# A gated mix of local attention and a spectral filter on one core: each engine's order planned anew

## The chip, the cores and the metric

The kernel runs on one core of a Trainium2 chip. The metric is the device time of one execution in microseconds (us), the median of several. The profile is of one execution; its times are in us from the first instruction. The engines are named as in the profile: PE (TensorE) multiplies matrices and PEld is its loading of weights, DVE (VectorE) and POOL (GpSimd) do elementwise work and reductions, ACT (ScalarE) copies, scales and takes exponentials, SP (SyncE) issues transfers.

## The reference

```
g = sigmoid((x * gate_w).sum(-1))                       # x: 1 x 2048 x 640, float32
a = attention(x @ wqkv) @ wo                            # 32 heads of 20; row s sees rows s, s-2, ..., s-14
b = irfft2(rfft2(x) * (w_r + 1j * w_i))                 # over rows and columns
return g * a + (1 - g) * b
```

The attention is over eight rows at distance two, with a softmax; rows before the start are masked.

## The kernel before

The 2048 rows are laid out as 128 partitions by 16 columns j, row 16p + j. Attention at distance two couples only columns of one parity, so even and odd j are two halves (`par` 0 and 1).

**Products of the input.** `qkv(par, hg)` multiplies eight column blocks of x, turned, by a quarter of `wqkv`. Each float32 factor is split into a rounded high part and a remainder, `hi` and `lo`, and three products are added. The names are `xe` and `xo` for the split x of even and odd j, `st` for the raw x of the first ones, `raw` and `w` for the weights before and after the split. ACT makes `hi`, DVE or POOL the `lo`. ACT evacuates the sums to `ev`, and its queue stores them in `qkvd` in device memory.

**Attention.** `attend(par, h)` loads `kt`, `q` and `vt` for a half of four heads, multiplies q by eight shifted rows of k (`pr`, on DVE with q copied to PSUM by ACT as `qbank`, or for some on POOL), reduces (`L`), takes the softmax, multiplies by v on POOL (`pv`), reduces on DVE (`o`) and stores to `od`.

**Spectral filter.** `fold(q)` loads x as `fx` and folds its columns on DVE; `cols` makes the first transform over rows (`z`). `freq(g)` runs for 16 groups of frequencies: `u` and `v` on PE, their sum and difference `ab` on DVE, `xa` to `xd` on PE, the filter on POOL (`P`) and DVE (`p`, `xd`, then `s`), and `g` on PE. The chain of one group on DVE is p, two operations on xd, two on s, each reading the one before. `spatial(j)` makes the way back (`oa`, `ob`, `ha`, `hb`, `y`).

**Projection.** `project_even` and `project_odd` load `ot` from `od`, turn it on PE (`oTp`), split it (`oT`) and multiply by `wo` into `woa` and `wob`, 15 products each. The even ones go by device memory (`ad`, read again as `yi`); the odd ones are the last work of the kernel, with the store of `out`.

**The order.** No engine's order is written out by hand. Every call on an engine is recorded by the class `Plan` (`record`, line 222) with its reads and writes (`touch`, line 188), and at the end `issue` (line 463) hands the calls out in the order that `order` (line 276) found. So all work is issued from L636 in the profile. `cost` (line 241) gives each operation its booked time `busy` and a latency `lat`. `forward` (line 411) is a simulated run in which each engine takes, of the operations that are ready, the one with the longest remaining path (`tail`). `backward` (line 369) recomputes `tail` from the end of that run. `turns` (line 315) repeats both, and `late` (line 329) judges an order by its end under three draws of random delays. `order` then tries 60 sets of tails with random shifts, one shift for each tile's name, and keeps the best. On the chip each engine runs its line strictly in the order found and waits for data where it isn't there.

Transfers are booked by a common link of 380 GB/s (`RATE`), a ring of 250 GB/s for each issuing engine (`QUEUE`) and a latency `LAND`. A load of an input may not start before `early`, which is 130 us (`AHEAD`) ahead of the time that its remaining path calls for. An operation behind one that it reads, on the same engine, is booked without a pause.

Of the kernel before, what the change touches and what calls it, by code (L numbers as in the profile page):

```python
# [139 lines left out]


class Op:
    __slots__ = ("i", "eng", "name", "call", "busy", "lat", "size", "preds", "succs", "chain", "tail", "start", "end", "early", "group", "of", "two")


class Engine:
# [9 lines left out]
class Plan:  # L156
# [31 lines left out]
    def touch(self, op, ap, write):  # L188

        if not hasattr(ap.tensor, "tag"):  # L190
            return
        tag, name = ap.tensor.tag, ap.tensor.name
        place = self.places.setdefault(tag, [name, {}, set()])
        if place[0] != name:
            assert name not in self.past, f"{name} used again after {place[0]}"
            self.past.add(place[0])
            self.places[tag] = place = [name, {}, {acc[0] for page in place[1].values() for acc in page}]
        pages, before = place[1:]
        if write:
            op.preds |= before  # L200
        p0, p1, idx = self.region(ap)
        size = PAGE if p1 > 1 else 1 << 30
        for pg in np.unique(idx // size):
            mine = idx[idx // size == pg]
            lo, hi, dense = mine[0], mine[-1], len(mine) == mine[-1] - mine[0] + 1
            kept = []
            for acc in pages.get(pg, ()):
                o, w, q0, q1, alo, ahi, adense, aidx = acc
                hit = o is not op and q0 < p1 and p0 < q1 and alo <= hi and lo <= ahi
                if hit and not (dense and adense):  # L210
                    hit = len(np.intersect1d(mine, aidx, assume_unique=True)) > 0
                if hit and (w or write):
                    op.preds.add(o)
                covered = write and hit and p0 <= q0 and q1 <= p1
                if covered:
                    covered = lo <= alo and ahi <= hi if dense else len(np.setdiff1d(aidx, mine, assume_unique=True)) == 0
                if not covered:
                    kept.append(acc)
            kept.append((op, write, p0, p1, lo, hi, dense, mine))
            pages[pg] = kept  # L220

    def record(self, eng, name, fn, a, k):
        op = Op()
        op.i, op.eng, op.name, op.chain, op.group = len(self.ops), eng, name, self.chain, self.group
        op.preds, op.succs, op.size, op.early, op.two = set(), [], 0, False, False
        line = sys._getframe(2).f_lineno
        code = self.code.get(line)
        if code is None:
            code = self.code[line] = compile("\n" * (line - 1) + "fn(*a, **k)", __file__, "exec")
        op.call = (code, {"fn": fn, "a": a, "k": k})  # L230
        aps = [v for v in list(a) + list(k.values()) if hasattr(v, "tensor") and hasattr(v, "ap")]
        out = k["out"] if "out" in k else a[0]
        ins = [v for v in aps if v is not out]
        for v in ins:
            self.touch(op, v, False)
        self.touch(op, out, True)
        op.of = out.tensor.name
        self.cost(op, out, ins, k)
        self.ops.append(op)

    def cost(self, op, out, ins, k):
        n = max(int(np.prod(v.shape[1:])) for v in [out] + ins[:1])
        if op.name == "dma_start":
            op.busy, op.lat = {"SP": 0.45, "ACT": 0.45, "POOL": 1.0}[op.eng], LAND
            op.size = int(np.prod(out.shape)) * 4
            op.early = not hasattr(ins[0].tensor, "tag")
        elif op.eng == "PE":
            n = int(np.prod(out.shape[1:]))
            if op.name == "transpose":
                op.busy = 0.109  # L250
            elif ins[-1].dtype == F32R:
                op.busy = n / 2400 + 0.018
            else:
                op.busy = 4 * n / 2400 + 0.006
            op.lat = 0.25
        elif op.eng == "DVE":
            op.busy, op.lat = 0.075 + n / 960, 0.12
            two = sum(v.tensor.tag[:4] not in ("bank", "qban") for v in ins) == 2
            if op.name == "scalar_tensor_tensor":
                op.busy += 0.06  # L260
            elif op.name == "reciprocal":
                op.busy += n * 0.007
            elif two:
                op.two = True
        elif op.eng == "ACT":
            strided = any(len(v.ap) > 2 and v.ap[-1][0] > 1 for v in [out] + ins)
            op.busy, op.lat = 0.12 + n * (1.75e-3 if strided else 0.78e-3), 0.15
            if len(ins) > 1:
                op.busy += 0.1
        else:  # L270
            spread = any(v.ap[-1][0] == 0 for v in ins)
            op.busy, op.lat = 0.09 + n * (2e-3 if spread else 2.25e-3), 0.14
        if op.eng in ("DVE", "ACT", "POOL") and not op.size:
            op.busy *= PACE

    def order(self):
        ops = self.ops
# [14 lines left out]
            last[key] = op  # L292
        span = max(op.tail for op in ops)
        for op in ops:
            op.early = max(0.0, span - op.tail - AHEAD) if op.early else 0.0
            op.tail += BIAS.get(op.chain, 0.0)
        rng = np.random.default_rng(SEED)
        self.draws = [rng.exponential(size=len(ops)).tolist() for _ in range(DRAWS)]
        best = self.turns(TURNS)

        names = {n: i for i, n in enumerate(dict.fromkeys(op.of for op in ops))}
        family = np.array([names[op.of] for op in ops])
        for _ in range(AGAIN):
            move = MOVE * rng.choice([0.3, 1.0, 2.0]) * rng.normal(size=len(names))
            move *= rng.random(len(names)) < rng.choice([0.1, 0.5, 1.0])
            for op, t in zip(ops, (best[1] + move[family]).tolist()):
                op.tail = t
            best = min(best, self.turns(2), key=lambda b: b[0])
        self.ends = best[0], best[3]
# [19 lines left out]
    def late(self, order, draw):  # L329

        line = {e: [op for op in order if op.eng == e] for e in ENGS}
        at, free, rings, link = dict.fromkeys(ENGS, 0), dict.fromkeys(ENGS, 0.0), dict.fromkeys(ENGS, 0.0), 0.0
        over, out = {}, {}
        head = {}
        last = 0.0
        for _ in range(len(order)):
            for e in ENGS:
                if head.get(e) is None and at[e] < len(line[e]):
                    op = line[e][at[e]]
                    t = free[e]  # L340
                    for q in op.preds:
                        if q not in out:
                            break
                        t = max(t, over[q] if q.eng == e and not q.size else out[q])
                    else:
                        head[e] = t
            e = min((h for h in ENGS if head.get(h) is not None), key=lambda h: head[h])
            op, t = line[e][at[e]], head.pop(e)
# [4 lines left out]
            over[op] = free[e] = end = t + busy  # L353
            if op.size:
                link = max(link, end) + op.size / RATE
                own = rings[e] = max(rings[e], end) + op.size / QUEUE
                end = (own if own >= link else min(link, own + op.size / QUEUE)) + SOONEST + LATER_BY * late
            else:
                end += op.lat - LATE.get(op.chain, 0.0)
            out[op] = end  # L360
# [3 lines left out]

    @staticmethod
    def lag(op, s):
        return 0.0 if s.eng == op.eng and not op.size else op.lat + EDGE.get((op.eng, s.eng), 0.0)

    def backward(self, end):

# [40 lines left out]
    def forward(self):  # L411
# [1 line left out]
        lat = self.lag  # L413
        wait = {op: len(op.preds) for op in ops}
        ready, pend = {e: [] for e in ENGS}, {e: [] for e in ENGS}
        free, rings, link = dict.fromkeys(ENGS, 0.0), dict.fromkeys(ENGS, 0.0), 0.0
        for op in ops:
            op.start = op.early
            if not wait[op]:
# [2 lines left out]
        while len(done) < len(ops):  # L422
# [26 lines left out]
            free[e] = op.end = op.start + op.busy  # L449
            avail = op.end  # L450
            if op.size:
                link = max(link, op.end) + op.size / RATE
                own = rings[e] = max(rings[e], op.end) + op.size / QUEUE
                avail = own if own >= link else min(link, own + op.size / QUEUE)
            done.append(op)
            for s in op.succs:
                wait[s] -= 1
# [9 lines left out]
                exec(*op.call)  # L467


TURNS, AGAIN, MOVE, SEED = 6, 60, 2.0, 2  # L470
DRAWS, SOONEST, LATER_BY = 3, 2.4, 0.6
ENGS = ("PE", "DVE", "ACT", "POOL", "SP")
RATE = 380e3
QUEUE = 250e3
LAND = 3.2
LATE = {"w": 1.0, "f": 4.0, "x": 3.5, "swap": 1.5}
AHEAD = 130.0
WAIT = 1.3
PACE = 1.02
EDGE = {("POOL", "ACT"): 2.0, ("DVE", "ACT"): 1.0}  # L480
LOOK = {"PE": 0.1, "DVE": 0.3, "ACT": 0.2, "POOL": 0.3, "SP": 0.0}
BIAS = {"first": 5.0, "logits": -5.0}
# [694 lines left out]
```

## Time and profile before

| | |
|---|---|
| median of 3 runs | 467.32 us (467.08 to 467.43) |
| span of the profiled execution, first to last instruction | 465.3 us |
| busy PE, DVE, POOL, ACT | 457.0, 423.4, 323.9, 205.2 us |
| moved by transfers | 105.90 MB, mean 228 GB/s |

The profiled execution's time is given by its span; the runs' median stands 2.0 us above it. Busy time of an engine is the time in which one of its instructions runs. Matmuls overlap, and their ends are modelled, so a short wait of PE can be hidden in its busy time; PEld, the loading of weights, shows such waits too. In a line such as `PE xb L636 <- DVE s L636: 1.2, 3, 0.7`, PE waited before xb for DVE's s, 1.2 us in all, three times, 0.7 us at most. In the chain of waits each row has a start, a length and what ran. Rows of the timeline give the start, the time from the first start to the last end, the engine, the operation and the count. Elementwise instructions overlap at their ends, so that a sequence's spacing is shorter than the time shown for one.

### The profile page before, as it was taken

The page shows a single profiled execution, that of the slowest core. Times are in us where ns is not written, and L with a number is a line of the kernel's source. Part 1 is how long each engine was busy: PE and PEld are TensorE (multiplying, and loading weights), DVE is VectorE, ACT ScalarE, POOL GpSimd, SP SyncE. Part 2 cuts the span into 40 slices and gives each one's busy share as a digit, 9 for nine tenths or more (in the row PEclk, how much of TensorE's full clock was granted, in tenths as well). Part 3 has the DMA queues.
Part 4 walks back from the last instruction along what each step waited for, and adds up shares of the span by engine and source line. Part 5 has one row for each costly group of instructions (what it writes and reads, how often), then busy time and mean ns, then how long its engine had stood idle before and what let it go on. Part 6 is the DMA issues. An engine that isn't in the chain of part 4 may idle for free.

```text
span 465.3 us, 7240 instructions
## 1 busy us (share of the span) xinstructions
PE 457.0 (98%) x2497; PEld 399.5 (86%) x2497; DVE 423.4 (91%) x555; ACT 205.2 (44%) x539; POOL 323.9 (70%) x264
## 2 busy tenths in 40 slices
PE   7999999999999999999999999999999999999997
PEld 4788888888889888899887788898888999988996
DVE  4699959999999999998999999999999997989784
ACT  5523346533335453257356465545444564333110
POOL 1003847999999879988698996767877997952300
PEclk9999999999999999999999999999999999999999
DMA  8999998796877968959998466567543321447732
GB/s 310 403 376 308 393 381 314 230 299 197 242 216 252 322 187 275 282 167 276 343 258 307 135 217 220 185 183 234 182 129 120 103 80 56 136 141 220 227 113 85
DMA packets 71700, 105.90 MB, mean 228 GB/s; under 512 B 20704, under 2 KB 50400, under 8 KB 71664
## 3 DMA queue, kind: packets, MB, share of 16 engines
q1 hardware_dynamic: 40624, 69.90, 46.0%
q10 hardware_dynamic: 30128, 31.55, 20.9%
q0 software_dynamic: 912, 4.00, 2.1%
q8 instruction: 19, 0.31, 0.3%
q14 instruction: 17, 0.14, 0.1%
HBM read 72.59 MB, written 32.84 MB: 227 GB/s over the span
## 4 chain that ended last, share of the span: by engine, by line
PE 82%; DVE 10%; DMA 4%; issue 2%; ACT 0%; ACTq 0%; DVEq 0%
PE qkv L636 43%; PE wob L636 6%; PE woa L636 6%; PE z L636 4%; PE ob L636 4%; PE oa L636 4%; PE u L636 2%; PE v L636 2%; PE hb L636 2%; PE g L636 2%; PE ha L636 2%; DVE xd L636 2%; DMA fx<-in_x 2%; PE oTp L636 2%; DVE s L636 1%
## 5 line engine op out<-in xcount | busy, mean ns | idle before, releaser
L636 PE MATMUL qkv<-w,xo 128*128 128x480 f32 (+1 forms) x480 | 110.7, 384 | 0.0
L636 PE MATMUL qkv<-w,xe 128*128 128x480 f32 (+1 forms) x465 | 104.1, 382 | 1.1 <-DVE xe L636 0.7
L636 PEld LDWEIGHTS qkv<-w,xe 128*128 128x128 f32 x465 | 87.3, 188 | 17.1 <-ACT xe L636 1.8
L636 PEld LDWEIGHTS qkv<-w,xo 128*128 128x128 f32 x480 | 89.8, 189 | 13.7
L636 ACT COPY ev<-qkv 128x480 f32<-128x480 f32 x64 | 35.4, 558 | 71.9 <-PE qkv L636 60.9
L636 PE MATMUL woa<-wo,oT 128*128 128x320 f32 x240 | 51.2, 317 | 0.1
L636 PE MATMUL wob<-wo,oT 128*128 128x320 f32 x240 | 50.4, 314 | 0.0
L636 PEld LDWEIGHTS wob<-wo,oT 128*128 128x128 f32 x240 | 39.0, 188 | 0.8 <-ACT ya L636 0.2
L636 PEld LDWEIGHTS woa<-wo,oT 128*128 128x128 f32 x240 | 39.0, 188 | 0.7 <-ACT oT L636 0.4
L636 POOL TENSOR_TENSOR w<-raw,w 128x480 fp32r<-128x480 f32 (+1 forms) x20 | 28.6, 1442 | 11.1 <-ACT w L636 11.1
L636 POOL TENSOR_TENSOR P<-X,wp 128x642 f32<-128x642 f32 x16 | 25.0, 1562 | 15.4 <-ACT X L636 15.4
L636 POOL DMA_DIRECT2D fd<-fx x6 | 4.3, 717 | 37.5 <-DMA raw<-in_wqkv 31.3
L636 POOL TENSOR_TENSOR yi<-yi,y 128x640 f32<-128x640 f32 x8 | 12.4, 1558 | 20.5 <-DMA yi<-ad 14.9
L636 ACT CAST oT<-oTp 128x384 fp32r<-128x384 f32 (+1 forms) x32 | 13.1, 427 | 29.9 <-PE oTp L636 25.2
L636 PEld LDWEIGHTS g<-mm,s 128*128 128x128 f32 x150 | 21.5, 191 | 3.6 <-ACT zg L636 0.2
L636 PE MATMUL g<-mm,s 128*128 128x128 f32 x150 | 22.7, 274 | 0.0
L636 PE MATMUL oa<-gt,zg 128*128 128x161 f32 (+1 forms) x96 | 22.1, 344 | 0.0
L636 PE MATMUL u<-bt,zc 128*128 128x321 f32 (+2 forms) x96 | 22.1, 344 | 0.0
L636 PE MATMUL v<-bt,zc 128*128 128x321 f32 (+2 forms) x96 | 22.1, 344 | 0.0
L636 PE MATMUL ob<-gt,zg 128*128 128x161 f32 (+1 forms) x96 | 21.0, 344 | 0.0
L636 ACT CAST w<-raw 128x480 fp32r<-128x480 f32 (+1 forms) x30 | 17.4, 594 | 7.4 <-DMA raw<-in_wqkv 2.2
L636 PEld LDWEIGHTS v<-bt,zc 128*128 128x128 f32 x96 | 16.3, 190 | 4.0 <-ACT vs L636 0.2
(301 smaller groups left out, 1118.7 us busy)
## 6 DMA issues: line engine op xcount, KB each, us to landing
qkvd<-ev ACTq DMA_DIRECT2D x32, 480.0 KB, 4.8
wp<-in_ws SPq DMA_DIRECT2D x16, 642.0 KB, 4.4
raw<-in_wqkv SPq DMA_DIRECT2D x25, 240.0 KB, 5.8
fx<-in_x SPq DMA_DIRECT2D x8, 641.0 KB, 9.0
ot<-od SPq DMA_DIRECT2D x16, 320.0 KB, 3.4
fd<-fx POOLq DMA_DIRECT2D x6, 640.0 KB, 8.5
f<-fd SPq DMA_DIRECT2D x6, 640.0 KB, 5.5
xt<-in_xT SPq DMA_DIRECT2D x8, 320.0 KB, 6.3
```

The source lines that it names most:

```text
L636: p.dve.memset(w, 0.0)
```

## The change

The change is in the planner and its constants alone; every computation and every transfer stays. The diff, without the two lines that declare fields and the deletion of the rings in the second simulation:

```diff
@@ record
-        ins = [v for v in aps if v is not out]
+        ins = [v for v in aps if v is not out] + [out] * (sum(v is out for v in aps) > 1)
@@ touch
                 if hit and (w or write):
                     op.preds.add(o)
+                    if not write:
+                        op.raw.add(o)
@@ cost
             elif ins[-1].dtype == F32R:
-                op.busy = n / 2400 + 0.018
+                op.busy = n / 2265 + 0.006
             else:
-                op.busy = 4 * n / 2400 + 0.006
+                op.busy = max(4 * n / 2400, 0.2) + 0.006
...
-            op.busy, op.lat = 0.075 + n / 960, 0.12
+            op.busy, op.lat = 0.061 + n / 960, 0.12
...
             if op.name == "scalar_tensor_tensor":
                 op.busy += 0.06
+                op.two = two
...
-            strided = any(len(v.ap) > 2 and v.ap[-1][0] > 1 for v in [out] + ins)
-            op.busy, op.lat = 0.12 + n * (1.75e-3 if strided else 0.78e-3), 0.15
+            near = any(v.tensor.tag[:4] in ("bank", "qban") for v in ins[:1])
+            op.busy, op.lat = (0.055 if near else 0.09) + n * 0.84e-3, 0.15
             if len(ins) > 1:
                 op.busy += 0.1
+            if any(v.offset >= 64 * v.ap[0][0] for v in [out] + ins):
+                op.busy += 0.13
         else:
             spread = any(v.ap[-1][0] == 0 for v in ins)
-            op.busy, op.lat = 0.09 + n * (2e-3 if spread else 2.25e-3), 0.14
-        if op.eng in ("DVE", "ACT", "POOL") and not op.size:
-            op.busy *= PACE
+            op.busy, op.lat = 0.05 + n * (1.97e-3 if spread else 2.3e-3), 0.14
@@ order
-            op.early = max(0.0, span - op.tail - AHEAD) if op.early else 0.0
+            op.input, op.early = op.early, max(0.0, span - op.tail - AHEAD) if op.early else 0.0
...
         best = self.turns(TURNS)
-
-        names = {n: i for i, n in enumerate(dict.fromkeys(op.of for op in ops))}
-        family = np.array([names[op.of] for op in ops])
-        for _ in range(AGAIN):
-            move = MOVE * rng.choice([0.3, 1.0, 2.0]) * rng.normal(size=len(names))
-            move *= rng.random(len(names)) < rng.choice([0.1, 0.5, 1.0])
-            for op, t in zip(ops, (best[1] + move[family]).tolist()):
+        for _ in range(2):
+            at = {op: t for op, t, _ in best[2]}
+            for op in ops:
+                if op.input:
+                    op.early = max(1.2 * (op.chain != "first"), min(at[s] for s in op.succs) - SOON - op.size / RATE)
+            for op, t in zip(ops, best[1].tolist()):
+                op.tail = t
+            best = self.turns(TURNS)
+
+        tiles, kinds = ([f(op) for op in ops] for f in (lambda op: op.of, lambda op: op.eng + op.of.rstrip("0123456789_+ab")))
+        tiles, kinds = (np.unique(k, return_inverse=True)[1] for k in (tiles, kinds))
+        for i in range(AGAIN):
+            move = np.zeros(len(ops))
+            for of, size, share in ((tiles, MOVE * rng.choice([0.3, 1.0, 2.0]), (0.1, 0.5, 1.0)), (kinds, WIDE * rng.choice([0.0, 0.3, 1.0]), (0.05, 0.2, 0.5))):
+                m = size * rng.normal(size=of.max() + 1)
+                m *= rng.random(len(m)) < rng.choice(share)
+                move += m[of]
+            for op, t in zip(ops, (best[1] + move).tolist()):
                 op.tail = t
             best = min(best, self.turns(2), key=lambda b: b[0])
@@ late
-                        t = max(t, over[q] if q.eng == e and not q.size else out[q])
+                        t = max(t, over[q] + (SAME.get(e, 0.0) if q in op.raw else 0.0) if q.eng == e and not q.size else out[q])
...
-                own = rings[e] = max(rings[e], end) + op.size / QUEUE
-                end = (own if own >= link else min(link, own + op.size / QUEUE)) + SOONEST + LATER_BY * late
+                end = link + SOONEST + LATER_BY * late
@@ lag
-        return 0.0 if s.eng == op.eng and not op.size else op.lat + EDGE.get((op.eng, s.eng), 0.0)
+        if s.eng == op.eng and not op.size:
+            return SAME.get(op.eng, 0.0) if op in s.raw else 0.0
+        return op.lat + EDGE.get((op.eng, s.eng), 0.0)
@@ constants
-TURNS, AGAIN, MOVE, SEED = 6, 60, 2.0, 2
+TURNS, AGAIN, MOVE, WIDE, SEED = 6, 150, 2.0, 15.0, 4
-RATE = 380e3
-QUEUE = 250e3
-LAND = 3.2
+RATE = 390e3
+LAND = 2.8
+SOON = 12.0
-PACE = 1.02
+SAME = {"DVE": 0.1, "ACT": 0.1, "POOL": 0.05}
```

In words: the booked times of PE, DVE, ACT and POOL operations are other numbers, and a DVE, ACT or POOL operation that reads the result of one on its own engine is booked to start 0.1 or 0.05 us after it. Transfers of all queues share one link of 390 GB/s, with no limit of a queue's own. After the first search, a load of an input may start no sooner than 12 us and its own transfer time ahead of the planned start of its first reader, and the search is repeated twice with that. Then 150 sets of shifted tails are tried instead of 60, with shifts by tile and by kind of operation, from another seed.

More of the change, by code (lines that the diff above doesn't have):

```diff
@@ L142 @@
 class Op:
-    __slots__ = ("i", "eng", "name", "call", "busy", "lat", "size", "preds", "succs", "chain", "tail", "start", "end", "early", "group", "of", "two")
+    __slots__ = ("raw", "input", "i", "eng", "name", "call", "busy", "lat", "size", "preds", "succs", "chain", "tail", "start", "end", "early", "group", "of", "two")
 class Engine:
@@ L224, in record @@
         op.i, op.eng, op.name, op.chain, op.group = len(self.ops), eng, name, self.chain, self.group
-        op.preds, op.succs, op.size, op.early, op.two = set(), [], 0, False, False
+        op.preds, op.raw, op.succs, op.size, op.early, op.two = set(), set(), [], 0, False, False
         line = sys._getframe(2).f_lineno
@@ L248, in cost @@
             n = int(np.prod(out.shape[1:]))
-            if op.name == "transpose":
+            if op.name == "transpose" or k.get("is_transpose"):
                 op.busy = 0.109
             elif ins[-1].dtype == F32R:
-                op.busy = n / 2400 + 0.018
+                op.busy = n / 2265 + 0.006
             else:
-                op.busy = 4 * n / 2400 + 0.006
+                op.busy = max(4 * n / 2400, 0.2) + 0.006
             op.lat = 0.25
         elif op.eng == "DVE":
-            op.busy, op.lat = 0.075 + n / 960, 0.12
+            op.busy, op.lat = 0.061 + n / 960, 0.12
             two = sum(v.tensor.tag[:4] not in ("bank", "qban") for v in ins) == 2
@@ L331, in late @@
         line = {e: [op for op in order if op.eng == e] for e in ENGS}
-        at, free, rings, link = dict.fromkeys(ENGS, 0), dict.fromkeys(ENGS, 0.0), dict.fromkeys(ENGS, 0.0), 0.0
+        at, free, link = dict.fromkeys(ENGS, 0), dict.fromkeys(ENGS, 0.0), 0.0
         over, out = {}, {}
@@ L415, in forward @@
         ready, pend = {e: [] for e in ENGS}, {e: [] for e in ENGS}
-        free, rings, link = dict.fromkeys(ENGS, 0.0), dict.fromkeys(ENGS, 0.0), 0.0
+        free, link = dict.fromkeys(ENGS, 0.0), 0.0
         for op in ops:
@@ L451, in forward @@
             if op.size:
-                link = max(link, op.end) + op.size / RATE
-                own = rings[e] = max(rings[e], op.end) + op.size / QUEUE
-                avail = own if own >= link else min(link, own + op.size / QUEUE)
+                avail = link = max(link, op.end) + op.size / RATE
             done.append(op)
```

## The prediction

> **What bounds the kernel now.** I read the page first, then the busy time by stage, then who kept TensorE waiting, then the chain of waits around the places where it stood.
>
> ```profile
> span 465.3 us, 7240 instructions
> ...
> PE 457.0 (98%) x2497; PEld 399.5 (86%) x2497; DVE 423.4 (91%) x555; ACT 205.2 (44%) x539; POOL 323.9 (70%) x264
> ```
>
> TensorE (PE) is busy 98% of the span, VectorE (DVE) 91%. The stages show where the rest lies (columns: stage, length, then busy time of PE, PEld, DVE, ACT, POOL, clock, DMA share, GB/s).
>
> ```profile
> 0.00:20.00 20.00, 17.06 (x62) 11.67 (x63) 9.03 (x15) 9.90 (x18) 1.99 (x9) 1.00 0.93 348
> 20.00:235.00 215.00, 214.84 (x1060) 187.22 (x1061) 204.42 (x202) 93.75 (x246) 167.05 (x129) 1.00 0.85 282
> 235.00:345.00 110.00, 108.76 (x617) 91.61 (x616) 107.19 (x166) 59.19 (x171) 88.42 (x77) 1.00 0.65 207
> 345.00:420.00 75.00, 75.00 (x479) 68.93 (x478) 69.47 (x96) 35.38 (x89) 60.28 (x47) 1.00 0.37 112
> 420.00:461.00 41.00, 40.49 (x282) 39.46 (x281) 32.74 (x79) 7.02 (x18) 6.20 (x4) 1.00 0.51 164
> 461.00:465.30 4.30, 0.88 (x6) 0.61 (x5) 0.55 (x1) 0.00 (x0) 0.00 (x0) 1.00 0.21 76
> ```
>
> PE idle is length less busy: 2.94, 0.16, 1.24, 0.00, 0.51 and 3.42 us, together 8.27. The granted clock is 1.00, so order alone is in question. The last 3.42 us are the last evacuation and its store; no order removes them. DVE has 2.8 us left in the third stage (110 less 107.19), which makes it the co-bound there. Who PE waited for, first by PE's own rows, then by its weight loads (PEld):
>
> ```profile
> PE xb L636 <- DVE s L636: 1.2, 3, 0.7
> PE warmed L636 <- DVE warm L636: 1.1, 1, 1.1
> PE qkv L636 <- DMA st<-in_xT: 0.9, 1, 0.9
> PE qkv L636 <- DVE xe L636: 0.7, 2, 0.6
> PE qkv L636 <- ACT xe L636: 0.4, 1, 0.4
> PE oTp L636 <- ACT h L636: 0.3, 1, 0.3
> ```
> ```profile
> PEld xb L636 <- DVE s L636: 2.1, 4, 1.0
> PEld qkv L636 <- ACT xe L636: 1.8, 3, 1.1
> PEld qkv L636 <- DVE xe L636: 1.4, 2, 0.9
> PEld oTp L636 <- DVE oT L636: 1.1, 4, 0.4
> PEld oTp L636 <- ACT h L636: 0.6, 1, 0.6
> ```
>
> The first six rows sum to 4.6 us. Two of them, 1.1 and 0.9, come before any data has landed and stay. What an order can win is therefore 2.6 us by PE's rows. A matmul's modelled end hides part of a wait, and by PEld's five rows it is 7.0; a load can wait while a matmul still runs, so the truth lies between.
>
> **The change part by part.** No instruction is added or removed: the same 2497, 555, 539 and 264 come in another order on each engine. So PE's work is the same, and only its waits move.
>
> *Durations.* The booked times against the trace:
>
> ```profile
> 20.68 118.98 PE qkv L636 x543
> ...
> 320.34 1.40 DVE pr5b L636
> 321.74 1.40 DVE L5b L636
> ...
> 457.48 2.21 PE woa L636 x15
> ```
> ```profile
> 36.12 1.02 ACT L636 COPY ev<-qkv 128x480 f32<-128x480 f32 x2 [0.91 <-DMA qkvd<-ev]
> ```
>
> One qkv matmul takes 118.98/543 = 0.219 us; booked before 480/2400 + 0.018 = 0.218, after 480/2265 + 0.006 = 0.218. A projection matmul takes 2.21/15 = 0.147; booked 0.151, now 0.147. A wide DVE operation takes 1.40 back to back; booked 1.02 x (0.075 + 1280/960) = 1.436, now 0.061 + 1.333 = 1.394. Two ACT copies of 480 take 1.02, which at 0.56 for the visible last one leaves 0.46 each; booked 0.504, now 0.458. The new numbers are nearer in three and equal in one, and the reserve on DVE is gone. By themselves they save nothing.
>
> *The pause between dependent DVE operations* (SAME, 0.1 us) is new. The longest stretch where DVE feeds PE, from the chain of waits:
>
> ```profile
> 342.54 0.41 DVE xd L636
> ...
> 342.98 0.51 DVE xd L636
> ...
> 343.58 0.90 DVE s L636 x2
> ...
> 344.52 0.81 PE xb L636 x2
> ```
>
> From the first xd to s are 1.04 us. Before, the planner booked two operations of 1.02 x (0.075 + 321/960) = 0.418, 0.84 together; now 0.395 + 0.395 + 2 x 0.1 = 0.99. Each of 16 groups was thus believed ready 0.2 us too early, which fits the PE waits on s. The booked error falls to 0.05. Term: of the 1.2 us by PE and 2.1 by PEld I take 1.0 as saved (bounds 0 and 2.1), nearer the PE row. What is late next there is DVE itself, with its 2.8 us.
>
> *Later input loads and one link.* The chain at the start, and the loads concerned:
>
> ```profile
> 11.10 7.44 DMA fx<-in_x
> ...
> 18.62 0.39 ACTq L636
> ...
> 19.05 0.73 ACT xe L636
> ...
> 19.80 0.84 DVE xe L636
> ...
> 20.68 3.33 PE qkv L636 x14
> ```
> ```profile
> 14.26 5.99 SPq L636 DMA_DIRECT2D fx<-in_x  x6
> ```
> ```profile
> 45.81 0.82 DVE L636 TENSOR_TENSOR fe<-fx 128x642 f32<-128x642 f32 x1
> ```
> ```profile
> fx<-in_x SPq DMA_DIRECT2D x8, 641.0 KB, 9.0
> ...
> qkvd<-ev ACTq DMA_DIRECT2D x1, 480.0 KB, 13.8
> ```
> ```profile
> DVE pr0a L636 <- ACT qbank L636: 4.2, 1, 4.2
> ```
>
> ACT's store issue at 18.62 sat behind an fx load that landed at 18.54, and the cast of the last xe queued behind it on ACT; PE waited for that. The last fold begins at 45.81, so its load is now held to 45.81 - 12 - 0.641/0.390 = 32.2 us, where all six were issued by 20.3. The SP queue issues the same loads, behind whatever stands before them, and the link is freer for the first qkvd store, which took 13.8 us. For PE the term is small: of the xe waits, 1.1 us by PE (3.2 by PEld), I take 0.5 (bounds: a loss of 1.0, if the cast queue is re-dealt badly, and 1.1). For DVE the 4.2 us wait at the first attention block can shrink. It is hidden now (PE has 214.84 of 215 in that stage), and costs nothing while PE's qkv work covers it; its use is that DVE enters the third stage further ahead. The other side: a load held to 12 us with 9.0 from issue to landing keeps 3.0 us of margin.
>
> ```profile
> 10.00:20.00 10.00, 9.39 (x40) 7.38 (x41) 5.63 (x9) 5.19 (x11) 0.00 (x0) 1.00 1.04 400
> ...
> 40.00:60.00 20.00, 20.00 (x93) 17.20 (x92) 18.54 (x24) 8.02 (x16) 13.60 (x10) 1.00 1.00 356
> ```
>
> The link carried 400 GB/s and 356 GB/s in two full stretches, so 390 for all queues together is fair at the start and 9% high later. The Trainium skill (DMA: Bandwidth & Descriptors, Specifications) speaks against the raised rate: it gives about 358 GB/s as the HBM limit of a core. By it landings in the first 20 us would be 8% or 1.6 us later than planned, the start's 0.5 would go, and my sum would be 1.1; the 400 of this trace disagrees.
>
> *The join at 421 us.* PE's wait for oTp is 0.3 by PE, 1.7 by PEld (1.1 + 0.6, four of them spread). I take 0.4.
>
> *The wider search* (150 perturbed plans, with moves by kind of operation) prices nothing itself; it can leave waits of its own in the stretch from 20 to 235 us that has 0.16 now, and in that from 345 to 420 with none. I take 0.3 us as a loss (bounds 0 and 1.9, the reserve worked out below).
>
> Sum: 1.0 + 0.5 + 0.4 - 0.3 = 1.6 us. The profiled span is 465.3, and the median of the runs 467.32 stands 2.0 above it, taken as unchanged around the span. Forecast 463.7 for the span and 465.7 for the time.
>
> The Trainium skill (Perfetto Trace Analysis, Identifying the Most-Contended Engine) says to judge TensorE's room by weight-load time and not by matmul time: 86%, so 65.8 us of room instead of 2.6 to 7.0. Where PE is full here, from 20 to 235 us, PEld shows 187.22 of 215, also 87%: that share is what saturation looks like, and I give the larger room no chance.
>
> **The rivals.** *Waits only move.* PE is full in two of the stages, and each engine's line is fixed, so a saved 1.2 us at xb can return elsewhere. Time 467.3, within 0.9. Against: the booked chain is now right. Chance 0.20.
>
> *All waits go.* 2.6 by PE, and a quarter of the 4.4 that PEld shows beyond it, 1.1: 3.7 us less, 463.6. Against: five small places must all come out well. Chance 0.12.
>
> *VectorE runs behind its plan, slower.* There are 64 + 64 + 54 wide DVE operations (16 attention blocks of four row pairs, each with two reduces and one multiply; ten multiplies are on POOL). The booking falls by 1.436 - 1.394 = 0.042 us on each, 7.6 us over the kernel, and some 1.9 of it in the third stage (by its 107.19 of 423.4 busy). The old surplus let DVE be ahead of the plan and PE's fixed order find its inputs ready. If the new plan spends it, PE stands at xb and at the evacuations for that time, and today's waits stay: 467.3 + 1.9 = 469.2. It decides once the plan leaves under 1.9 us between s or ab and PE's use of it. For it: DVE has 2.8 us in that stage. Against: the 0.1 us pauses give part back. Chance 0.18.
>
> *A bad start, slower.* The re-dealt ACT queue puts a wait on a transfer ahead of the xe casts, as at 18.62, but earlier: twice that wait's 0.7 us by DVE's row, 1.4 in all, 468.7. Chance 0.10.
>
> *The order barely changes.* Then the first rival holds; its chance is in that one.
>
> **How the numbers follow.** A difference under 0.2%, 0.9 us, can hardly be told from none. Forecast 0.40 and all waits 0.12 give faster 0.52; waits that move, 0.20, is the same; the two slower ones give 0.28. The range goes from 463.5, just under all waits gone, to 469.0, just short of the dearer slower case; by the cases it leaves out under 2 in 10. The likeliest case alone spans 464.7 (the 2.6 us of PE's rows saved) to 466.4 (0.9 saved).
>
> **What would show it.** Right: the same 7240 instructions, PE near 457 busy, the xb wait on s at a few tenths, fx issues spread to about 30 us, the first qkvd store landing in far less than 13.8 us, the 4.2 us wait at pr0a gone, idle from 20 to 235 us still under 0.5. Wrong: new PE waits of over 1 us in all between 235 and 420 us, with DVE over 98% busy there, or a first 20 us with over 3 us of PE idle. If DVE enters the third stage ahead and PE still waits for s, the cause was not the booked pause.

## The result and the profile after

| | before | after |
|---|---|---|
| median of four runs each | 467.2 us | 481.09 us (480.02 to 481.61) |
| ratio | | 1.029 (95%: 1.027 to 1.0309) |
| profiled execution: span | 465.3 us | 478.3 us (time 480.69) |

The forecast was 465.7 us. The changed kernel is 13.9 us slower, on the other side and outside the range. Here and below a run over 1.5% above the fastest of its kernel is left out of the median; that is one run each of e4, e7, e9 and e10, and with it their medians are 477.6, 476.7, 469.8 and 478.0 us, as some expectations quote them. The page of after, then its stages (columns as in the prediction):

```profile
span 478.3 us, 7260 instructions
...
PE 464.0 (97%) x2497; PEld 402.9 (84%) x2497; DVE 422.9 (88%) x555; ACT 206.3 (43%) x539; POOL 318.8 (67%) x264
...
PEclk9999999999979999999999999999999999999999
```
```profile
0.00:20.00 20.00, 17.98 (x60) 12.77 (x61) 12.69 (x20) 12.64 (x24) 1.99 (x9) 1.00 0.94 349
20.00:235.00 215.00, 208.86 (x1019) 181.43 (x1018) 200.90 (x198) 89.16 (x232) 161.76 (x129) 0.98 0.82 268
235.00:345.00 110.00, 108.45 (x594) 90.22 (x593) 107.46 (x158) 57.52 (x172) 90.28 (x79) 1.00 0.69 222
345.00:420.00 75.00, 74.51 (x466) 66.85 (x466) 60.11 (x83) 34.68 (x86) 56.83 (x44) 1.00 0.38 116
420.00:461.00 41.00, 40.33 (x270) 37.98 (x269) 35.29 (x86) 10.58 (x26) 7.89 (x5) 1.00 0.56 169
461.00:478.30 17.30, 13.90 (x97) 13.62 (x95) 6.41 (x14) 1.70 (x4) 0.00 (x0) 0.99 0.20 76
```

The instruction counts of the compute engines are those of before. PE idle by stage is 2.02, 6.14, 1.55, 0.49, 0.67 and 3.40 us: the start improved (2.94 before), and the stage that had 0.16 now has 6.14, with 41 matmuls fewer in it and a clock of 0.98. Who kept PE waiting, and the place of the largest wait on SP, on DVE and on PE:

```profile
PE z L649 <- DMA fc<-in_t_fc: 5.1, 1, 5.1
PE v L649 <- ACT vs L649: 1.5, 1, 1.5
PE warmed L649 <- DVE warm L649: 1.1, 1, 1.1
PE qkv L649 <- DMA st<-in_xT: 1.0, 1, 1.0
PE qkv L649 <- ACT ev L649: 0.9, 1, 0.9
```
```profile
131.25 0.36 SPq L649 DMA_DIRECT2D od<-o1a  x1
131.71 0.52 SPq L649 DMA_DIRECT2D kt3b<-qkvd  x1
132.32 0.87 SPq L649 DMA_DIRECT2D raw<-in_wqkv  x2
133.25 0.50 SPq L649 DMA_DIRECT2D fc<-in_t_fc  x1
```
```profile
129.75 1.48 DVE L649 TENSOR_REDUCE o1a<-pv1a 128x160 f32<-128x1280 f32 x1
```
```profile
125.80 7.37 PE L649 MATMUL qkv<-w,xo 128*128 128x480 f32 x33
138.28 0.77 PE L649 MATMUL z<-fc,fx 128*128 128x128 f32 x2 [5.11 <-DMA fc<-in_t_fc]
```
```profile
130.00:138.30 8.30, 3.19 (x16) 2.46 (x14) 8.17 (x7) 2.06 (x7) 8.30 (x8) 0.91 0.94 298
138.30:143.60 5.30, 5.30 (x18) 4.67 (x18) 5.26 (x6) 1.31 (x4) 5.10 (x5) 0.50 0.75 228
```

The table `fc` stands on SP behind the store of `o1a` and three other loads. That store could not go until VectorE's last reduce of `o1a` was done at 131.2, and the load landed when PE had stood for 5.11 us. Then TensorE ran at half clock, 0.50 over 5.30 us, which costs half of that, 2.65 us. The place is worth 7.8 us. It looks like the cause, and the first experiment shows that it isn't. All of PE's idle time grew by 6.0 us, from 8.27 to 14.27; with the half clock that is 8.7 of the 13.0 us by which the span grew. The rest lies in PE's busy time, 464.0 against 457.0 us, where modelled ends hide short waits; which waits these are isn't shown.

VectorE is late long before. ACT, SP and DVE between 44 and 65 us:

```profile
48.28 0.38 ACTq L649 DMA_DIRECT2D qkvd<-ev  x1
...
50.07 0.96 ACT L649 COPY qbank<-q0a 128x160 f32<-128x160 f32 x3
...
62.90 0.56 ACT L649 COPY ev<-qkv 128x480 f32<-128x480 f32 x1 [9.65 <-DMA qkvd<-ev]
...
63.91 0.28 ACT L649 COPY qbank<-q0b 128x160 f32<-128x160 f32 x1
```
```profile
44.21 1.64 SPq L649 DMA_DIRECT2D raw<-in_wqkv  x3
```
```profile
64.23 1.49 DVE L649 TENSOR_TENSOR pr0a<-kt0a,qbank 128x1280 f32<-128x1280 f32 x1 [7.24 <-ACT qbank L649]
```

The same multiply of before, on DVE:

```profile
62.91 1.49 DVE L636 TENSOR_TENSOR pr0a<-kt0a,qbank 128x1280 f32<-128x1280 f32 x1 [4.20 <-ACT qbank L636]
```

The store issued at 48.28 held its `ev` buffer until 62.9, 14.6 us, beside three `raw` loads issued from 44.21 on and other transfers. ACT's next `ev` copy waited 9.65 us for that buffer, and everything behind it on ACT waited too. VectorE's multiply waited 7.24 us for the `qbank` copy at 63.91, which carries `q0b`, although it reads a third of the tile that was written at 50.07 already. Before, that wait was 4.2 us.

**How late an engine is.** Each operation has a start that the planner booked. Its start in the trace less that booked start is called its lag here. It says nothing about where the time goes, but it shows when a kernel falls behind its own plan, and whether it catches up. The multiply at 64.23 was booked at 53.20, a lag of 11.0 us; the same multiply of before ran at 62.91, booked at 60.05, a lag of 2.9. So it ran only 1.3 us later than before, where the new plan had asked for it 6.9 us earlier. VectorE's mean lag over stretches of booked time, from one profiled execution each:

| kernel | 75 to 95 us | 222 to 240 us | last, from 430 us |
|---|---|---|---|
| before | 4.7 | 2.5 | 3.2 |
| after | 12.5 | 13.1 | 16.5 |

PE's lag in its last part (440 us on) is 3.1 and 16.5, the same as VectorE's. The planner's booked end is about the same for both, 463.3 and 462.4 us. So most of the loss is a lag that VectorE has by 64 us, 11.0 us at that multiply; it reached PE at 133 us, and then it grew to 16.5 us instead of falling. Between 90 and 240 us VectorE of after is full, with less room than before (VectorE alone, before and then after):

```profile
90.00:240.00 150.00, 146.06 (x129) 1.00 0.81 252
...
90.00:240.00 150.00, 148.70 (x130) 0.98 0.78 239
```

For the VectorE operations that start in this stretch, each up to the start of the next, the plan of after has 149.6 us and its trace 150.2; for before they are 152.9 and 150.6. The plan of before was longer than what VectorE needed, that of after a little shorter.

### The profile page after: what moved, and what is told of

Its sections match the earlier page's. It is cut to its first block, busy times and chain, and to the rows that moved or that the text cites. A ratio compares the mean times of both kernels' runs of the same rounds, so it can differ in the third digit from the quotient of the medians.

```text
span 478.3 us, 7260 instructions
## 1 busy us (share of the span) xinstructions
PE 464.0 (97%) x2497; PEld 402.9 (84%) x2497; DVE 422.9 (88%) x555; ACT 206.3 (43%) x539; POOL 318.8 (67%) x264
## 4 chain that ended last, share of the span: by engine, by line
PE 62%; DMA 4%; DVE 3%; ACT 1%; issue 1%; DVEq 0%; ACTq 0%; SPq 0%
PE qkv L649 15%; PE woa L649 7%; PE wob L649 7%; PE g L649 4%; PE oa L649 4%; PE ob L649 4%; PE v L649 3%; PE u L649 3%; PE z L649 2%; PE xa L649 2%; PE xd L649 2%; PE xc L649 2%; DMA qkvd<-ev 2%; PE hb L649 2%; PE xb L649 2%; PE oTp L649 2%
## 5 line engine op out<-in xcount | busy, mean ns | idle before, releaser
L649 PE MATMUL qkv<-w,xo 128*128 128x480 f32 (+1 forms) x480 | 116.1, 392 | 0.9 <-ACT ev L649 0.9
L649 PE MATMUL qkv<-w,xe 128*128 128x480 f32 (+1 forms) x465 | 102.3, 382 | 0.0
L649 PEld LDWEIGHTS qkv<-w,xo 128*128 128x128 f32 x480 | 90.3, 192 | 13.9 <-ACT ev L649 1.0
L649 PE MATMUL woa<-wo,oT 128*128 128x320 f32 x240 | 45.5, 316 | 0.3 <-ACT oT L649 0.3
L649 PE MATMUL wob<-wo,oT 128*128 128x320 f32 x240 | 45.1, 315 | 0.2 <-ACT ya L649 0.2
L649 POOL TENSOR_TENSOR w<-raw,w 128x480 fp32r<-128x480 f32 (+1 forms) x20 | 25.4, 1278 | 20.1 <-ACT w L649 20.1
L649 PEld LDWEIGHTS woa<-wo,oT 128*128 128x128 f32 x240 | 37.2, 188 | 1.0 <-ACT oT L649 0.6
L649 PEld LDWEIGHTS wob<-wo,oT 128*128 128x128 f32 x240 | 37.4, 188 | 0.8 <-ACT ya L649 0.4
L649 ACT CAST oT<-oTp 128x384 fp32r<-128x384 f32 (+1 forms) x32 | 13.1, 426 | 31.3 <-PE oTp L649 26.7
L649 PE MATMUL ob<-gt,zg 128*128 128x161 f32 (+1 forms) x96 | 22.6, 344 | 0.0
```

The costliest lines, as they stand in the source:

```text
L649: p.dve.memset(w, 0.0)
```

## The experiments

All kernels of this part do the whole computation. Times are medians; those of before in the same comparisons lie between 467.6 and 468.0 us. The first theories were T1, that the held `fc` load is the cause, and T2, that VectorE runs behind its plan from 50 us on.

**1. The table's load early; the multiplies regrouped.** The order of after, taken as found, with single moves:

```diff
 e1: SP's line
-od<-o1a, kt3b, raw, raw, fc
+fc ahead of the last loads of fx (issued at 14.2 us); the rest as it was
 e2: order of recording around block 0, every engine's own line unchanged
-qbank copy, pr0a4, ..., qbank copy, pr0a6, ..., pr0b0
+pr0a4, its sums and pr0a6 ahead of the first copy; pr0b0 ahead of the second
 e3: both
```

> The changed kernel with the order that its planner found on every engine, but for one transfer: SP issues the load of the table fc among the first loads, where the kernel before has it, and not behind the store of o1a. Theory T1 (the held table load is the cause): PE's wait of 5.1 us at 133 us goes, and with it the stretch of 6.8 us at half clock behind it, worth 3 us more; 481.1 falls by 8.4 to about 472.7. Theory T2 (VectorE runs 13 us behind its plan from 64 us on, and PE's line must wait for it somewhere): PE reaches the frequency stage 8 us earlier and waits there for DVE; the wait moves, the time stays at 479 to 481.

> The changed kernel with every engine's line the same, and only the order of recording between engines changed at one place: the third and fourth multiply of the first attention block stand ahead of ACT's next copies into qbank, so that they no longer wait for a copy that they don't read. DVE's idle time of 7.2 us at 57 to 64 us should fall by about 5.8, to under 2. T1: the table load follows DVE on the SP queue, so it comes 5.8 us earlier and PE's 5.1 us wait goes: about 472.7, as with the load alone. T2: everything behind DVE comes 5.8 us earlier: PE's wait at 133 us goes, and the later waits shrink too; 472 to 475, with DVE some 7 us behind its plan instead of 13.

> Both edits together: table load early, and the two multiplies ahead of the copies. T1: nothing beyond the table load alone, about 472.7. T2: the table load adds nothing to the other edit, which gives what it gives alone, 472 to 475; if both causes count in turn, below each alone, about 470.

Measured: e1 483.4, e2 476.7, e3 478.0 us. With the table there in time the kernel isn't faster; PE's list in e1 shows why:

```profile
PE qkv L658 <- ACT ev L658: 6.5, 1, 6.5
PE z L658 <- ACT ev L658: 2.4, 2, 1.4
PE xa L658 <- DVE p L658: 1.2, 1, 1.2
```

The lag surfaces at the next place where PE needs ACT or VectorE: 10.1 us in these three rows in place of 5.1, and the half clock is there again (0.50 from 150.1 to 156.9 us). T1 falls. Regrouping took VectorE's lag from 12.5 to 7.6 us at 75 to 95 us (e2), and some 4 us of the time, but at 222 to 240 us it was 12.7 again, and 17.2 at the end. The profiled execution of e2 took 480.9 us, 4.2 above its median, so its last two lags are high; e3, profiled near its median, has 8.2, 10.5 and 13.6 and grows too. So the wait at `pr0a` brings some 5 us of the lag and is not what keeps the rest. Neither theory had the times of e2 and e3, 475 us at most by both.

**2. One part taken back at a time.** The remaining theories: D, that the fitted durations took away VectorE's reserve; L, that transfers are booked too short and loads are held into the stretch of the stores; and an unlucky draw of the search.

```diff
 e4: the two rounds that hold the loads left out
-        for _ in range(2): ... op.early = ... - SOON - op.size / RATE ...
 e5: durations, reserve and pauses of before
-            op.busy, op.lat = 0.061 + n / 960, 0.12      (and the others)
+            op.busy, op.lat = 0.075 + n / 960, 0.12
+            op.busy *= PACE                              (1.02; no SAME)
 e6: the two-part booking of transfers of before
+                own = rings[e] = max(rings[e], op.end) + op.size / QUEUE   (RATE 380e3, LAND 3.2)
 e7: another draw
-TURNS, AGAIN, MOVE, WIDE, SEED = 6, 150, 2.0, 15.0, 4
+TURNS, AGAIN, MOVE, WIDE, SEED = 6, 150, 2.0, 15.0, 2
 e8: new durations with a reserve on DVE, ACT and POOL, transfers of before, loads not held
+            op.busy *= 1.03
```

> The changed planner without the two rounds that hold input loads to 12 us before their first reader; durations, one link and wider search stay, and a new order comes out. T1: with no load held there is no late table, 472.7 or less. T2: transfers are still booked too short and DVE still without reserve, so DVE again falls 8 us or more behind its plan by 100 us, and the time stays above 475.

> The changed planner with the booked times of engines as before (1.02 x the old formulas, no pause between dependent operations); one link, held input loads and the wider search stay; a new order comes out. The first run showed that the table load alone is not the cause (483.4, no gain), so the question is which booking puts VectorE behind its plan. Theory D (durations without reserve): DVE falls behind at the start as in the changed kernel, but catches up by 3 us or more between 90 and 230 us, as it does in the kernel before; 470 to 475. Theory L (transfers booked too short, and loads held into the same stretch): the lag of 11 us at 64 us stays, and with it the time, 477 or more.

> The changed planner with transfers booked as before (link of 380 GB/s, ring of 250 GB/s for each issuing engine, latency of 3.2 us); new durations, held input loads and the wider search stay. L: attention is planned some 4 us later, DVE's lag at 64 us is under 6 us and the time falls to 470 to 474. D: the lag at 64 us is smaller, but never made good, it grows by 4 us or more to the end, and the time stays at 474 or more.

> The changed planner with the seed of the search as before (2, not 4), all else as changed. Both D and L: the bookings are at fault, another draw gives another order with the same fault, DVE 10 us or more behind its plan at the end, 475 to 485. Rival (an unlucky draw): a time near the kernel before, 465 to 470.

> New durations with the pause between dependent operations, but times 1.03 on DVE, ACT and POOL, transfers booked as before, no held loads, the wider search. D and L together: DVE's lag stays under 6 us from 64 us to the end and PE waits little; 464 to 470, so about as before or a little faster. If neither booking is the cause, 475 or more.

Measured: e4 475.8, e5 471.0, e6 473.7, e7 475.0, e8 471.9 us. The two kernels with a reserve are the fastest. All three without it stay at 473.7 and above, whatever else was taken back. VectorE's lag goes with it: from 75 to 95 us to 222 to 240 us it falls from 7.4 to 2.6 in e5 and from 7.7 to 4.5 in e8, and stays in e6, 7.9 and 8.0. But e8 missed its range, 464 to 470 us, and is only 1.8 us ahead of e6, less than two new orders can differ (experiment 4); e6 alone took 7.4 us off, so L wasn't excluded.

**3. The reserve alone, and the other parts alone.**

```diff
 e9: after, one line more, for VectorE only
         elif op.eng == "DVE":
             ...
+            op.busy *= 1.03
 e10: before with the wider search alone (150 draws, WIDE, SEED 4)
 e11: before with the two holding rounds alone
 e12: before, its own lines, pr0a4 recorded ahead of the later qbank copies
```

> The changed kernel with only VectorE's booked durations 3% longer (ACT and POOL without reserve, one link, held loads and wide search stay). D (the missing reserve on VectorE keeps a lag that the transfers of 42 to 64 us cause): VectorE starts late as in the kernel after, but makes 3% of its 300 us between 90 and 400 us good; 470 to 474 us, VectorE's lag behind the planner's starts falls by over 4 us from 90 to 240 us. L (transfers booked too short are all that counts): the lag stays, 476 to 481 us. Unlucky draw: anything within 468 to 481, with no fall of the lag.

> The kernel before with only the wider search (150 draws over two kinds of shifts, 4 for the seed); durations, link and loads as before. D and L both: the search by itself costs nothing that the reserve does not make good; 465 to 470 us, and the lag falls between 90 and 240 us. A theory that the wider search itself gives an order with less give in it: 472 us or more.

> The kernel before with only the two rounds that hold each input load to 12 us ahead of its planned first reader. D: the reserve makes good what late loads cost; 466 to 470 us. L: the loads then lie with the stores of 42 to 64 us and the table's load ends late for z, as in the kernel after; 471 to 478 us, with a TensorE wait of over 2 us for an input load and stores of over 12 us in the profile.

> The kernel before with its own order on every engine, only five of the multiplies and sums of block 0 recorded ahead of the later copies into other thirds of the same tile, so that they do not wait for these. It takes away VectorE's wait of 4.2 us at 57 to 62 us. D (with a reserve a lag of some us is made good before anything reads it): the same time as before within 0.3%, 466.3 to 469 us, although VectorE waits about 4 us less. A theory that every us VectorE waits there comes out at the end: 463 to 464.5 us.

Measured: e9 469.7, e10 477.8, e11 472.2, e12 467.7 us (e12 against before: 1.0002, 95% 0.9984 to 1.002). One factor on one engine took 11.4 us off the changed kernel. The disturbance is still there; in e9 ACT and DVE read:

```profile
53.48 1.02 ACT L650 COPY ev<-qkv 128x480 f32<-128x480 f32 x2 [10.91 <-DMA qkvd<-ev]
```
```profile
DVE pr0a L650 <- ACT qbank L650: 7.5, 1, 7.5
```

while its stages, SP and PE show that little of it comes out:

```profile
20.00:235.00 215.00, 213.03 (x1051) 185.38 (x1050) 202.45 (x199) 90.89 (x240) 163.05 (x130) 1.00 0.83 272
```
```profile
130.60 0.42 SPq L650 DMA_DIRECT2D fc<-in_t_fc  x1
```
```profile
139.97 0.27 PE L650 MATMUL z<-fc,fx 128*128 128x128 f32 x1
```

ACT waits 10.91 us for a store and VectorE 7.5 us, about as long as in after (9.65 and 7.24); yet PE stands 1.97 us in this stage, not 6.14. The table's load, held as in after, is issued 9.4 us ahead of its reader. The expectation of a fall by over 4 us between 90 and 240 us was missed: VectorE's lag fell by 1.2 (7.6 to 6.4), so the gain is also a smaller lag at 75 to 95 us and none added later.

e10 went against D. Its bookings hold the old reserve, and it lost all the same, at two places (ACT, then PE):

```profile
19.87 0.72 ACT L639 CAST xe<-st 128x640 fp32r<-128x640 f32 x1 [3.25 <-DMA fc<-in_t_fc]
...
247.46 1.02 ACT L639 COPY ev<-qkv 128x480 f32<-128x480 f32 x2 [3.47 <-DMA qkvd<-ev]
```
```profile
20.64 3.57 PE L639 MATMUL qkv<-w,xe 128*128 128x482 f32 x10 [2.47 <-ACT xe L639]
...
249.46 0.81 PE L639 MATMUL v<-bt,zc 128*128 128x321 f32 x2 [3.15 <-ACT vs L639]
```

Both times ACT stood for a transfer with work behind it that PE needed at once. Behind each of the two waits TensorE ran at half clock for 3.42 us (0.50 from 21.67 to 25.09 and from 250.36 to 253.78 us), which costs 3.4 us together; with the 5.6 us of waits that is 9.0 of the 10 us that e10 is slower than before. With a wait so near its reader, VectorE's reserve has no stretch in which to make it good; that is how I read it, and no run tests it.

e11 lies in L's range by its time, but not by its signs: PE waits for no input load by over 0.9 us.

e12 gained nothing, but doesn't test what it was made for: the multiply ran early, and the next one waited instead (DVE):

```profile
58.52 1.48 DVE L645 TENSOR_TENSOR pr0a<-kt0a,qbank 128x1280 f32<-128x1280 f32 x1
...
64.88 1.49 DVE L645 TENSOR_TENSOR pr0a<-kt0a,qbank 128x1280 f32<-128x1280 f32 x1 [3.36 <-ACT qbank L645]
```

**4. How far one order lies from another.** New draws with nothing else changed:

```diff
 e13, e14: before
-TURNS, AGAIN, MOVE, SEED = 6, 60, 2.0, 2
+TURNS, AGAIN, MOVE, SEED = 6, 60, 2.0, 1      (e14: 3)
 e15: e9 with SEED 2;  e16: e10 with SEED 2
```

> The kernel before with 1 in place of 2 for the seed of its search, all else as before. D (the reserve decides): any order that the old durations give makes its lag good, 466 to 471 us. S (the order of before was a fortunate draw, and any new order costs some us, reserve or not): 471 to 480 us.

> The kernel before with 3 for the seed, all else as before: a second draw of the same kind. D: 466 to 471 us. S: 471 to 480 us. The distance between this, the first draw and before is the spread that a single new order has by itself; a difference between two orders that is smaller than this spread can't be put down to the edit between them.

> The changed kernel with VectorE's booked durations 3% longer, as in the run that took 469.8 us, and 2 in place of 4 for the seed. D: 468 to 474 us, against 476.7 us for the same seed without the reserve. S: the 469.8 us was a fortunate draw, 474 to 481 us.

> The kernel before with only the wider search, 2 in place of 4 for the seed (4 took 478.0 us). D: 466 to 472 us, the 478.0 us was an unfortunate order at 18 and 247 us. S: 472 to 480 us. A theory that the wider search itself gives orders with less give: 474 to 480 us with the two runs of the narrow search below it.

Measured: e13 469.2, e14 470.8, e15 468.1, e16 469.2 us. Three draws of before lie within 467.8 and 470.8, so a single order has a spread of about 3 us. The two draws of the wider search, e10 and e16, lie 8.6 us apart, so with it a single pair of orders proves little. The order of before is the best of its three. The reserve holds in the second draw too: 475.0 without, 468.1 with it, and e15 can't be told from before (1.0008, 95% 0.9986 to 1.003). Its stages:

```profile
20.00:235.00 215.00, 214.39 (x1058) 186.89 (x1057) 205.04 (x201) 91.94 (x244) 164.26 (x132) 1.00 0.86 279
235.00:345.00 110.00, 110.00 (x624) 91.96 (x622) 106.43 (x171) 59.95 (x172) 89.92 (x78) 1.00 0.68 220
```

The wider search isn't to blame by itself: the 477.8 of e10 became 469.2 in e16 by the draw alone.

**5. With the reserve, held loads or not.**

```diff
 e17: e9 without the two holding rounds
 e18: the same with SEED 2
```

> The changed kernel with VectorE's booked durations 3% longer and without the two rounds that hold input loads; new durations, one link, pause and wide search stay. D with L as its smaller part (held loads bring the lag about, the reserve makes it good): 464 to 469 us, VectorE's lag at 64 us under 6 us, and under 4 us at 235 us. A theory that holding the loads counts for nothing once the reserve is there: 468 to 472 us, as with the held loads (469.8 and 468.1 us for two seeds).

> The same with 2 in place of 4 for the seed. D with L: 464 to 469 us. Held loads count for nothing: 467 to 471 us. Two draws each with and without held loads stand beside the spread of some 3 us of the kernel before with three seeds; only a difference above that counts.

Measured: e17 469.1, e18 472.1 us, against 469.7 and 468.1 with held loads. The difference is inside the spread, in both directions: what the holding costs once the reserve is there can't be seen. D with L also missed e17's lag, under 6 us at 64 us and under 4 at 235: it was 9.9 and 7.1. No version was found that beats before.

VectorE's lag in the pairs that differ by the factor 1.03 alone:

| pair | time | lag 75 to 95 us | 222 to 240 us | from 430 us |
|---|---|---|---|---|
| after, e9 | 481.1, 469.7 | 12.5, 7.6 | 13.1, 6.4 | 16.5, 7.5 |
| e7, e15 (second draw) | 475.0, 468.1 | 8.3, 5.4 | 11.8, 3.4 | 14.6, 3.2 |
| e4, e17 (loads not held) | 475.8, 469.1 | 5.8, 9.9 | 7.6, 7.1 | 10.7, 11.1 |

The times differ by 11.4, 6.9 and 6.7 us. As ratios to before, measured beside each, the 95% intervals are 1.027 to 1.0309 and 1.0018 to 1.0056 for the first pair, 1.0131 to 1.0217 and 0.9986 to 1.003 for the second, 1.0116 to 1.0239 and 1.0009 to 1.0046 for the third; no pair's two overlap. The first lag differs by the order, the next by what VectorE does with it: without the reserve the lag rose by 0.6, 3.5 and 1.8 us from the first to the second stretch, with it it fell by 1.2, 2.0 and 2.8. In the third pair the profiled executions have nearly the same span (471.2 and 471.4 us) and lag at the end, so there only the medians tell the two apart. Over all 20 kernels: the seven without a reserve (four orders, since e1 to e3 keep that of after but for single moves) took 473.7 to 483.4 us, twelve of the thirteen with one 467.2 to 472.2, and e10 477.8. From the first to the second stretch the lag rose in all seven without, by 0.1 to 5.1 us, and fell in eleven of the thirteen with one, by 0.5 to 4.8; it rose in e10 (6.3 to 6.4) and e16 (3.3 to 6.0). As any new booking also gives a new order, the evidence is that three pairs of three go the same way and that the two groups hardly overlap, not the size in one pair.

## Why the prediction was wrong

*Durations: this is the step that failed.* The fit was read rightly, 1.394 booked against 1.40 measured, and the text even said that "the reserve on DVE is gone". It then concluded "By themselves they save nothing" and put 0 into the sum. Three pairs of orders put the reserve at 11.4, 6.9 and 6.7 us, each with the spread of its draws in it. A booking that is 3% too long isn't a cost that a fit takes away. In a stretch where VectorE is 99% busy it is the only rate at which a lag is made good: 3% of 150 us or some 4.5 us between 90 and 240 us as an estimate, of which the pairs showed a fall by 1.2, 2.0 and 2.8 us. The planner booked 418.0 us of VectorE before and 402.0 after, 16 us less; the prediction counted 7.6 of it, on the wide operations.

*The rival "VectorE runs behind its plan, slower"* named the right engine and was priced at 1.9 us, with its place between s and PE's use in the third stage. It counted on VectorE of before being ahead of its plan; VectorE was 2.5 to 4.7 us behind it and made part of that good. And the rival had no disturbance to make good. The real one was at 44 to 64 us, in a stage that the prediction called covered, and left a lag of 11 us; it first came out at 133 us through SP's line. The 0.28 for slower was too little.

*Later input loads and one link.* "3.0 us of margin" for a held load was reckoned from its issue to its landing alone. The load of `fc` lost its margin in SP's line, behind a store that waits for VectorE, which the prediction didn't look at for that load. The term 0.5 for the start came out, 2.94 to 2.02 us of idle. The wait of 4.2 us at `pr0a`, which "can shrink", grew to 7.24. Held loads aren't shown to cost anything with the reserve there (experiment 5); alone on before they gave 472.2, 1.4 us above its draws, which is left open. So is the booking of one link: e6 took 7.4 us off without a reserve, and no pair with one differs by it alone.

*The pause.* PE's waits for `s`, 1.2 us, are gone after, as the term of 1.0 had it. In the larger loss it can't be seen in the time, and e5, without the pause, also has none in PE's rows.

*The join at 421 us* gave nothing: idle 0.51 before, 0.67 after.

*The wider search.* The 0.3 us was too small as a size of what one order may differ by: three draws of the narrow search span 3.0 us, two of the wide one 8.6.

*What would show it* worked in part. There were 7260 instructions and not 7240, though with the same counts for PE, DVE, ACT and POOL. The `fx` issues ended at 23 us and not at 30, and the first `qkvd` store still took 12.5 us (18.66 to 31.18) where 13.8 was to shrink far. New PE waits of over 1 us after 235 us were there (v, 1.5), but VectorE's share from 235 to 345 us was 97.7%, not over 98%, and the main loss was in the stage before, where idle was to stay under 0.5 and was 6.14.

Left open: how much of each pair's difference is the reserve and how much the draw, and why the lag at 75 to 95 us differs from order to order; the lag of each kernel is from one execution.

## What to carry to other kernels

A fixed order can need a reserve on the engine that is nearly full, as this one did: price its removal as the lag that can no longer be made good, and look for the disturbance anywhere upstream, not at the places where the engine feeds the bound. The largest wait in a profile may be only the first place where a lag comes out; take it away and see whether the time goes with it. Where an order comes from a search, draw it anew a few times before putting a difference down to an edit.

## What the hardware showed that was not expected

- In the wait of 5.11 us the granted clock fell to half at 136.8 us, 3.6 us after the last matmul, and it stayed at 0.50 until 143.6 us, 5.3 us of matmuls included. The Trainium skill (TensorE: Matmul & The Clock Gate, Part 1: The HAM clock gate) states that at least one idle window of about 3.4 us halves the clock and at least one such window of sustained work restores it. The trace of after agrees with both. That of e10 doesn't on the first: waits of only 2.47 and 3.15 us were enough there, so the measurement goes before the page; the half clock came 1.0 and 0.9 us after the matmuls had resumed, for 3.42 us each. In the 3.42 us ahead of it PE was busy for 1.02 and 0.90 us.
- A 480 KB store took 14.6 us to give its buffer back beside loads; the median of all 32 is 5.2 us by the page.

```profile
qkvd<-ev ACTq DMA_DIRECT2D x32, 480.0 KB, 5.2
```

- How much the runs of one order differ depends on the order: seven runs of before beside e4 lie between 467.33 and 468.12 us, three of e4 between 472.97 and 479.30, seven of e17 between 466.78 and 473.21. That an order without a reserve varies more isn't shown.
